# Another written order of an attention and mixer kernel: the second batch's sums of values go ahead of the first channel mix, and twelve clamps and three scalings run on GpSimd

## The chip, the cores and the metric

One core of a Trainium2 chip runs the kernel. The metric is the device time of one execution in microseconds, the median of several runs.

## The reference, cut to what matters

Linear attention (4 batches, 4 heads, 1088 rows, 32 columns a head) feeds a mixer: a token mix over the 1088 rows, then a channel mix from 128 to 1536 columns and back, each with a residual.

```python
def phi(x):                       # r = 8, so 64 features from 32 columns
    a = np.einsum('rd,bhsd->bhsr', S1, x)
    b = np.einsum('rd,bhsd->bhsr', S2, x)
    return np.einsum('bhsi,bhsj->bhsij', a, b).reshape(*x.shape[:-1], r * r)
q_p, k_p = (phi(q), phi(k))
kv = np.einsum('bhsf,bhsd->bhfd', k_p, v)
z = np.sum(k_p, axis=2)
num = np.einsum('bhsf,bhfd->bhsd', q_p, kv)
den = np.einsum('bhsf,bhf->bhs', q_p, z)[..., None] + 1e-06
x = (num / den).transpose(0, 2, 1, 3).reshape(B, S, H * D)
h = np.maximum(x.transpose(0, 2, 1) @ w_tok1, 0.0) @ w_tok2
u = x + h.transpose(0, 2, 1)
return u + np.maximum(u @ w_ch1, 0.0) @ w_ch2
```

## The kernel before, in words

**The order.** The program first adds some 1050 operations to a plan, each with the engines that may run it, and then emits them in the order of the string `ORDER` (`Plan.run`). An entry `w02.clamp:pool` names an operation and, behind the colon, its engine (`dve` is VectorE, `act` ScalarE, `pool` GpSimd; without one, the first engine that the operation lists). Each engine works through its own instructions in this order, so an entry's place counts only against entries of the same engine: TensorE, VectorE, ScalarE, GpSimd, or SP, which issues the loads (`d00` alone is issued by ScalarE) and all other transfers. Semaphores between the engines are set from what the instructions read and write. Tiles rotate through a fixed number of buffers in the order of the string (`ps_a` 3 PSUM banks, `ps_h` 3, `ps_o` 2, `o_sb` 2), so an operation that takes a buffer waits until the last reader of the tile before in it is done.

**The weights.** They arrive as 64-bit floats and are converted on the core. Weight 0 is `w_tok1` in six pieces (256, 256, 512, 512, 512 and 256 columns), 1 is `w_tok2` in six (384 four times, 320 twice), 2 and 3 are `w_ch1` and `w_ch2` in four each (256, 256, 512, 512). `dWI` loads piece I of weight W. Then `convert` runs six operations: `abs` scales the high words into `c` (L270 on VectorE or GpSimd, L272 on ScalarE), `low` turns the low words into `tail` (L276, ScalarE), `sign` takes the sign bits (L281 on ScalarE, into a bank of `ps_h`; L284 on VectorE, in place), `clamp` bounds `c` (L287), `merge` joins `c` and the sign (L290, VectorE), `add` adds `tail` (L294, L296, GpSimd). `hi` and `lo` (L377 ScalarE, L380) split a piece into two halves that TensorE multiplies at its fast rate; pieces of weights 2 and 3 need them before the channel mix, those of 0 and 1 before batch 1's token mix. `s` is the same for S1 and S2.

**A batch.** `qB`, `kB`, `vB` load the inputs. `K.p0`, `p4` project the keys (L407), `K.c0`, `c4` copy one factor (L418, ScalarE), `K.v0`, `v4`, `v8` form the products (L428, VectorE: 1024, 1024 and 256 columns), and `K.s` sums values over them (L448: 72 short matmuls as six operations for batch 0, 144 as one for the others); `K.kvz` copies the sums (L457). `Q0` projects and multiplies batch 0's queries on the chip (`p`, `a`, `m`: L537, L559, L569); for the others `Q.p` projects (L497), `Q.c0`, `c1` copy, `Q.w0`, `w1` write the rows to DRAM, `Q.r..` read them back spread out, and `Q.m..` multiply (L632). `A.x` attends (L652, 24 short matmuls a third; batch 0 as `x0` to `x2`), `A.d0` to `d2` divide (L663, L664, L666, VectorE), `A.t0` to `t2` are the first token matmuls (L702 or L708), `A.relu` (L720), `A.hT` transposes (L742), `A.hTh`, `hTl` split, `A.u0` to `u2` put x into the bank (L733, batch 0), `A.w0` to `w2` are the second token matmuls (L824 or L828); for batches 1 to 3 x goes through DRAM (`xb`, `xm`, `xT`) and `us` adds it. `A.uhIK` and `A.ulIK` split u into halves for span K (L799, L802).

**The channel mix.** The 4352 rows are cut into 12 spans, `U0` to `U11`, of 384, 320 or 288. A span has 12 blocks of 128 hidden columns, and each block four operations: `f`, three matmuls into a bank of `ps_h` (L878); `h`, the relu to `hh` (L882, ScalarE); `l`, the rest `hl` (L885, VectorE), which frees the bank; `s`, three matmuls into the span's bank of `ps_o` (L891). `U2.f#4` below is the fourth block's `f`. `oh`, `ol` and `out` add u and store. `f` of blocks 1 and 2 needs piece 20, of 3 and 4 piece 21, of 5 to 8 piece 22, of 9 to 12 piece 23; `s` the same of weight 3.

**Fills.** `fill:n` emits n bfloat16 matmuls of 512 columns that nobody reads (L248); eight stand ahead of the whole string. Before the change the string has seven.

## Time and profile before

| | us |
|---|---|
| three runs | 217.52, 217.95, 216.55 |
| their median | 217.52 |
| the profiled execution | 218.62 |
| its span, first to last instruction | 216.8 |

The profile is of one execution. Times in it are from the span's start; the other 1.8 us of that execution lie around the span. PE is TensorE's matmuls, PEld its weight loads, which overlap them; DVE is VectorE, ACT ScalarE, POOL GpSimd. A matmul of two 32-bit operands shows as two records. A granted clock of 1.00 is 2.4 GHz on TensorE, and matmuls at half of it take twice their time.

### The profile page before, as it was taken

The page shows a single profiled execution, that of the slowest core. Times are in us where ns is not written, and L with a number is a line of the kernel's source. Part 1 is how long each engine was busy: PE and PEld are TensorE (multiplying, and loading weights), DVE is VectorE, ACT ScalarE, POOL GpSimd, SP SyncE. Part 2 cuts the span into 40 slices and gives each one's busy share as a digit, 9 for nine tenths or more (in the row PEclk, how much of TensorE's full clock was granted, in tenths as well). Part 3 has the DMA queues.
Part 4 walks back from the last instruction along what each step waited for, and adds up shares of the span by engine and source line. Part 5 has one row for each costly group of instructions (what it writes and reads, how often), then busy time and mean ns, then how long its engine had stood idle before and what let it go on. Part 6 is the DMA issues. An engine that isn't in the chain of part 4 may idle for free.

```text
span 216.8 us, 5259 instructions
## 1 busy us (share of the span) xinstructions
PE 209.7 (97%) x2069; PEld 195.0 (90%) x2069; DVE 144.9 (67%) x305; ACT 118.7 (55%) x282; POOL 64.5 (30%) x73
## 2 busy tenths in 40 slices
...
PEclk9999999799999999999999999999999999999999
...
GB/s 229 399 407 399 402 357 204 194 179 248 29 216 242 197 165 17 108 186 238 182 101 0 3 3 60 172 61 0 30 5 2 42 36 3 24 0 0 51 0 54
DMA packets 11472, 28.44 MB, mean 131 GB/s; under 512 B 1336, under 2 KB 5432, under 8 KB 11448
## 3 DMA queue, kind: packets, MB, share of 16 engines
...
q8 instruction: 16, 0.26, 0.5%
q10 hardware_dynamic: 144, 0.26, 0.4%
...
## 4 chain that ended last, share of the span: by engine, by line
PE 87%; DMA 4%; DVE 2%; issue 2%; SPq 2%; ACT 1%; ACTq 0%
PE ps_h L878 34%; PE ps_o L891 33%; DMA doubles<-wt 4%; PE ps_a L708 4%; PE ps_a L828 4%; PE ps_a L652 3%; PE ps_a L448 2%; PE ps_a L824 2%; SPq L252 1%; PE ps_a L702 1%; PE ps_a L407 1%; DVE c L290 1%; PE ps_a L497 1%; DVE k_p L428 1%; PE ps_a L733 1%
## 5 line engine op out<-in xcount | busy, mean ns | idle before, releaser
L885 DVE SCALAR_TENSOR_TENSOR hl<-ps_h,hh 128x384 fp32r<-128x384 f32 (+2 forms) x144 | 74.9, 532 | 59.6 <-ACT hh L882 58.5
L882 ACT ACTIVATE hh<-ps_h 128x384 fp32r<-128x384 f32 (+2 forms) x144 | 67.7, 475 | 75.4 <-PE ps_h L878 54.5
L878 PE MATMUL ps_h<-uh,halves 128*128 128x384 f32 (+2 forms) x288 | 87.6, 335 | 0.0
L891 PE MATMUL ps_o<-hh,halves 128*128 128x384 f32 (+2 forms) x288 | 71.5, 330 | 0.0
L878 PEld LDWEIGHTS ps_h<-uh,halves 128*128 128x128 f32 x288 | 53.8, 190 | 1.0 <-ACT hh L882 0.4
L891 PEld LDWEIGHTS ps_o<-hh,halves 128*128 128x128 f32 x288 | 50.6, 189 | 0.2
L878 PE MATMUL ps_h<-ul,halves 128*128 128x384 f32 (+2 forms) x144 | 47.7, 331 | 0.0
L891 PE MATMUL ps_o<-hl,halves 128*128 128x384 f32 (+2 forms) x144 | 47.3, 328 | 0.0
L878 PEld LDWEIGHTS ps_h<-ul,halves 128*128 128x128 f32 x144 | 27.4, 190 | 0.2 <-DVE ul L802 0.2
L891 PEld LDWEIGHTS ps_o<-hl,halves 128*128 128x128 f32 x144 | 27.2, 189 | 0.0
L802 POOL TENSOR_TENSOR ul<-us,uh 128x320 fp32r<-128x320 f32 (+3 forms) x8 | 6.6, 821 | 57.6 <-ACT uh L799 47.4
L294 POOL TENSOR_TENSOR whole<-c,tail 128x384 int32<-128x384 int32 (+3 forms) x12 | 11.8, 995 | 9.1 <-DVE c L290 7.8
L676 POOL TENSOR_TENSOR xl<-x,xh 128x384 fp32r<-128x384 f32 x7 | 7.1, 1019 | 22.6 <-ACT xh L672 22.6
L632 POOL TENSOR_TENSOR qp<-qp,br 128x544 f32<-128x544 f32 x8 | 10.9, 1369 | 6.2 <-PE ps_o L891 4.5
L428 DVE TENSOR_TENSOR k_p<-ps_a,a_sb 128x1024 f32<-128x1024 f32 (+1 forms) x12 | 11.4, 950 | 0.5 <-ACT a_sb L418 0.4
L276 ACT ACTIVATE tail<-doubles 128x256 int32<-128x256 uint32 (+3 forms) x20 | 10.9, 552 | 0.7 <-DMA doubles<-wt 0.7
L652 PEld LDWEIGHTS ps_a<-kvz,qp 128*64 128x64 f32 x288 | 8.9, 137 | 2.0 <-issue 0.9
L652 PE MATMUL ps_a<-kvz,qp 128*64 128x66 f32 x288 | 9.8, 223 | 0.5 <-issue 0.3
L290 DVE SCALAR_TENSOR_TENSOR c<-c,ps_h 128x512 int32<-128x512 int32 (+3 forms) x17 | 9.3, 559 | 1.1 <-ACT ps_h L281 0.8
L708 PE MATMUL ps_a<-halves,xh 128*128 128x256 f32 x54 | 9.9, 280 | 0.0
L281 ACT ACTIVATE ps_h<-doubles 128x512 int32<-128x512 f32 (+3 forms) x17 | 9.2, 543 | 0.0
L380 POOL TENSOR_TENSOR halves<-whole,halves 128x384 fp32r<-128x384 f32 (+3 forms) x7 | 8.1, 1177 | 2.4 <-ACT halves L377 2.4
...
## 6 DMA issues: line engine op xcount, KB each, us to landing
...
```

Of the source, the lines that this page charges most:

```text
L276: nc.scalar.activation(t["tail"], low.bitcast(U32), AF.Copy, scale=2.0 ** -29)
L281: nc.scalar.activation(t["sign"], f32(high), AF.Prelu, scale=2.0 ** -19, alpha=2.0 ** 70)
L290: nc.vector.scalar_tensor_tensor(t["c"], t["c"], 3, t["sign"], op0=ALU.logical_shift_left, op1=ALU.bitwise_or)
L294: engines[e].tensor_tensor(dst(), t["c"], t["tail"], op=ALU.add)
L428: nc.vector.tensor_tensor(t["k_p"][:pn, t0 * H:t1 * H], a.unsqueeze(3).broadcast_to([pn, n, R, R]), t["sb", base][:pn, at:at + n].unsqueez ...
L632: engines[e].tensor_tensor(qp[:, p, cs], qp[:, p, cs], t["br"][:, p, cs], op=ALU.mult)
L652: nc.tensor.matmul(x_ps[c:c + 64, o:o + 2 * (D + 1)], lhsT=qp[:, p, s0 + c:s0 + c + 64], rhs=kvz_all[b % 2][:, p, :], start=True, stop=True,)
L708: nc.tensor.matmul(t["h_ps"][:, :DTOK], lhsT=t[l][:m, i, :], rhs=part(0, piece, r, j * DTOK, DTOK)[:m], start=(i == 0 and k == 0), stop=(i ...
L878: nc.tensor.matmul(h_ps[:, :cn], lhsT=part(2, at[2][e][0], l, at[2][e][1] * P, P), rhs=r[:, :cn], start=(m == 0), stop=(m == 2))
L882: nc.scalar.activation(t["hh"][:, :cn], t["h"][:, :cn], AF.Relu)
L885: nc.vector.scalar_tensor_tensor(t["hl"][:, :cn], t["h"][:, :cn], 0.0, f32(t["hh"][:, :cn]), op0=ALU.max, op1=ALU.subtract)
L891: nc.tensor.matmul(outs[i][:, :cn], lhsT=part(3, at[3][e][0], l, at[3][e][1] * P, P), rhs=r[:, :cn], start=(e == 0 and m == 0), stop=(e == ...
```

## The change

Only the string `ORDER` is changed. The work is the same but for the fills, of which the string now has nine, one at a time but for the first four, and for the engines of some operations:

- Scalings (`abs`): w02 goes from GpSimd to ScalarE; w00 from VectorE, w10 and w23 from ScalarE to GpSimd; w01 and w33 from VectorE to ScalarE; w03, w13, w22 and w31 from ScalarE to VectorE.
- Clamps: w01, w10, w03, w04, w13, w11, w32, w14 and w23 go from VectorE to GpSimd, w00 and w33 from GpSimd to VectorE; with w02, w05 and w20, which stay there, GpSimd has twelve.
- Signs: those of s, w00 and w15 go to ScalarE, of w01 and w23 to VectorE; Q0.s0 goes from GpSimd to VectorE.
- Halves: `lo` of w22, w23, w13, w05 and some of the later `A.l` and `A.ul` go to VectorE; `lo` of w00, w04 and w12, some `A.ul` and Q3.m00, m01 go to GpSimd; `oh` of spans 0 and 2 goes to GpSimd, of span 1 to VectorE.

On TensorE K1.s now stands between A0.w0 and A0.w1, ahead of the first U0.f; A0.x0 ahead of Q1.p; K1.p0 and p4 between A0.t0 and A0.t1; A0.u2 behind the first U0.f. On SP the order of the loads changes: k0 ahead of d10 and v0, d14 to the end with d33, and v1 behind Q1.w0 but ahead of d32, d23, q2 and d15. Cut to the part up to the second batch, and the end:

```diff
--- before.py
+++ after.py
@@ -61,53 +61,53 @@
 ORDER = """
-d00 s d10 q0 s.low s.abs w00.low w00.abs:dve s.sign:dve s.clamp s.merge s.add w00.clamp:pool Q0.s0:pool w00.sign:dve w00.merge w00.add w10.abs:act
-w10.low Q0.s1:act d01 w10.clamp:dve w10.sign:act w10.merge w01.abs:dve w10.add w01.low fill:4 Q0.p00 Q0.p01 Q0.a00 Q0.a01 w01.sign:act Q0.m00 Q0.m01
-w01.clamp:dve w01.merge Q0.p20 Q0.a20 k0 d02 K0.p0 K0.p4 Q0.p21 K0.c0 s.rows w02.abs:pool w02.clamp:pool K0.c4 w02.low Q0.a21 d04 w02.sign:act v0
-K0.v0 Q0.m20 K0.v8 Q0.m21 K0.v4 d03 q1 d05 fill:2 Q0.p10 Q0.p11 K0.s00 K0.s04 K0.s08 K0.s10 K0.s14 K0.s18 w04.abs:act Q0.a10 Q0.a11 w04.low w01.add
-w02.merge w02.add w04.clamp:dve Q0.m11 Q0.m10 w03.abs:act w03.low w04.sign:act K0.kvz w03.clamp:dve w05.abs:dve w05.clamp:pool w04.merge w03.sign:act
-Q1.p d13 w03.merge Q1.c0 w05.low Q1.c1 w13.abs:act w05.sign:act w13.low w13.sign:act A0.x0 w04.add d11 d12 d30 d20 k1 d21 d22 d14 d31 d32 q2 d23 v1
-Q1.w0 Q1.w1 d15 d33 w03.add A0.d0 A0.x1 w13.clamp:dve w05.merge A0.d1 w13.merge w05.add A0.x2 A0.t0 A0.d2 A0.t1 A0.t2 w11.abs:act w11.low w12.low
-w12.abs:act w30.abs:act w11.sign:act w30.low w12.sign:act w30.sign:act A0.relu w13.add K1.p0 A0.hT K1.p4 w11.clamp:dve w20.abs:dve w12.clamp:dve
-w30.clamp:dve w11.merge w12.merge w30.merge w20.clamp:pool w11.add w20.low K1.c0 w20.sign:act w12.add w30.add w21.abs:act w21.low K1.c4 A0.hTh
-w21.sign:act w22.low w30.hi K1.v0 w20.merge w20.add w20.hi w20.lo:pool w22.abs:act K1.v4 w21.clamp:dve w30.lo:dve K1.v8 w21.merge fill:1 A0.u0 A0.u1
-A0.w0 A0.w1 A0.uh00 w22.sign:act w31.abs:act A0.ul00 w22.clamp:dve w14.abs:dve U0.f U0.f Q2.p w21.add w21.hi w21.lo:pool w22.merge w22.add A0.uh11
-A0.ul11 U1.f U0.h w31.low U0.l U0.h U0.l w32.low w32.abs:act w31.clamp:dve w31.sign:dve w14.clamp:dve w32.clamp:dve w31.merge U1.h w22.hi w32.sign:act
-U1.l w32.merge w31.add w14.low w31.hi w14.sign:act Q2.c0 U0.s U0.s w14.merge K1.s U0.f U0.f U1.s w22.lo:pool w31.lo:pool w32.add U0.h w15.low U0.h
...
-U10.h U10.l U10.h U10.l U11.f U11.f U10.s U11.h U11.l U11.h U11.l U11.h U11.l U11.f U10.s U11.h U11.l U11.f U11.s U10.f U11.s U10.f U11.s U11.s U11.h
-U11.l U10.h U10.l U10.h U10.l U10.f U10.h U10.l U11.f U11.s U10.s U11.f U11.f U10.s U11.h U11.l U10.s U11.f U11.h U11.h U11.h U11.l U11.l U10.ol U11.l
-U11.s U11.f U11.h U11.s U11.s U11.s U11.l U11.s U11.ol U10.out U11.out
+d00 s q0 d01 k0 s.abs s.low s.sign:act w00.low s.clamp w00.abs:pool w00.clamp:dve s.merge s.add Q0.s0:dve Q0.s1:act w00.sign:act s.rows w01.abs:act
+w01.low w00.merge fill:4 Q0.p00 Q0.p01 Q0.a00 Q0.a01 Q0.p20 Q0.a20 d10 w01.clamp:pool w01.sign:dve w01.merge Q0.m00 Q0.m01 K0.p0 K0.p4 Q0.p21 K0.c0
+Q0.a21 w10.low K0.c4 K0.v0 K0.v4 w01.add w00.add w10.abs:pool w10.clamp:pool fill:1 Q0.p10 v0 d02 w10.sign:act d05 d03 d04 w10.merge K0.v8 Q0.m21
+w05.abs:dve Q0.m20 K0.s00 K0.s04 K0.s08 K0.s10 K0.s14 K0.s18 Q0.p11 q1 d12 d13 k1 d11 w02.abs:act w02.low Q0.a11 w02.sign:act w03.low Q0.a10 w10.add
+w02.clamp:pool w05.clamp:pool K0.kvz w05.low w04.abs:act w02.merge w03.abs:dve Q0.m10 Q0.m11 w05.sign:act w03.sign:act w04.low fill:1 A0.x0 A0.d0
+fill:1 Q1.p Q1.c0 Q1.c1 w04.sign:act w03.clamp:pool w05.merge w02.add w04.clamp:pool A0.x1 w03.merge w05.add w03.add A0.d1 w04.merge w12.abs:act
+w13.abs:dve w12.clamp:dve w13.clamp:pool w13.low w12.low w13.sign:act w12.sign:act A0.x2 A0.t0 A0.d2 d21 d20 d30 d31 d22 Q1.w0 v1 d32 d23 q2 d15 Q1.w1
+d14 d33 Q1.r0None Q1.r00 Q1.r01 Q1.r1None Q1.r10 Q1.r11 fill:1 K1.p0 K1.p4 w04.add w13.merge K1.c0 w11.low w11.abs:act K1.c4 w11.sign:act w12.merge
+K1.v0 w13.add w11.clamp:pool w20.abs:dve w12.add w20.clamp:pool w20.low w20.sign:act w30.low w30.abs:act A0.t1 A0.t2 A0.relu fill:1 A0.hT w21.low
+w11.merge w11.add K1.v4 w20.merge K1.v8 w20.add A0.hTh A0.u0 A0.u1 A0.w0 K1.s A0.w1 w30.sign:act w20.hi w21.abs:act w22.abs:dve w30.clamp:dve
+w30.merge w22.low w21.sign:act w31.low A0.uh00 w22.sign:act w20.lo:pool w21.clamp:dve w31.abs:dve w22.clamp:dve w31.clamp:dve w31.sign:dve w30.add
+K1.kvz w30.hi w32.low A0.uh11 w21.merge A0.ul00 w21.add w22.merge w31.merge w30.lo:dve U0.f A0.u2 U0.f A0.ul11 U0.h w32.abs:act U0.h w22.add
+w32.clamp:pool w31.add U0.l U1.f U1.f U0.l U0.s U0.s U1.h w21.hi w21.lo:pool U1.l U1.h w22.hi U1.l U1.s U0.f Q2.p U1.s w22.lo:dve w14.abs:dve
+w15.abs:dve w32.sign:act w31.hi w14.low U0.h w32.merge U0.l w14.clamp:pool w31.lo:pool w15.clamp:dve w14.sign:act w15.low w15.sign:act w14.merge U0.f
+w15.merge U0.s U1.f U1.f U0.h U1.h U0.l w32.add w14.add w15.add U1.l U0.f U0.s U0.f U1.h U1.l U0.h w05.hi w32.hi U0.l U0.h w23.low w02.hi Q2.c0 w04.hi
+U0.l w23.abs:pool w23.clamp:pool w23.sign:dve w23.merge w23.add U1.s U1.f U1.s A0.w2 U1.f U1.h w32.lo:dve U0.f U1.l Q1.m00:pool U0.s U1.s U0.f U0.s
+A0.uh22 U1.h Q2.c1 w33.low U1.l U0.h A0.ul22 U0.l U1.f U1.s U1.f U0.s w23.hi U0.h w23.lo:dve U0.l U0.f w13.hi U1.h U1.l Q1.m10:dve w33.abs:act w11.hi
+U1.h U0.h w00.hi w01.hi w33.clamp:dve U1.l U0.l U1.f U0.s U1.s U1.s U1.h w33.sign:act U1.l U0.f U1.f Q1.m01:dve Q1.m11:pool w33.merge w03.hi w15.hi
+U0.h U1.h w33.add w33.hi w33.lo:pool w04.lo:pool w02.lo:pool A1.x U1.l U0.l w01.lo:dve A1.d0 A1.d1 A1.d2 A1.xb U0.f U0.f U2.f U0.s U1.s U1.s U0.s
+Q2.w0 Q2.w1 v2 k2 q3 Q2.r0None Q2.r00 A1.xm Q2.r01 A1.xT0 A1.xT1 A1.xT2 Q2.r1None A1.xT3 Q3.p U0.h U0.h Q3.c0 A1.h0 U0.oh:pool w00.lo:pool w03.lo:pool
...
+U9.ol U9.out U11.f U10.s U11.f U11.h U11.l U10.s U11.f U11.h U11.l U11.s U11.h U11.l U11.f U11.f U11.s U11.s U11.f U11.h U11.l U11.h U11.l U11.h U11.l
+U11.s U10.f U11.f U11.s U11.s U11.f U10.h U10.l U11.h U11.l U11.h U11.l U10.f U10.f U11.s U10.s U10.h U10.l U10.h U10.l U11.s U11.f U10.s U11.f U11.f
+U10.s U11.h U11.h U11.l U11.l U11.f U11.h U11.h U11.l U10.ol U11.l U11.s U11.s U11.s U11.s U11.ol U10.out U11.out
 """.split()
```

## Rows read from the trace of the kernel before

**Rows 1.** The page's head: busy us (share of the span) and instructions of each engine, and the granted clock in 40 slices, in tenths.
```profile
PE 209.7 (97%) x2069; PEld 195.0 (90%) x2069; DVE 144.9 (67%) x305; ACT 118.7 (55%) x282; POOL 64.5 (30%) x73
...
PEclk9999999799999999999999999999999999999999
```
**Rows 2.** The cut into stretches: length in us, then each engine's busy us and instructions, the granted clock, the DMA engines' busy share and GB/s.
```profile
25.00:30.00 5.00, 4.80 (x38) 3.18 (x39) 4.80 (x10) 5.00 (x15) 4.33 (x6) 1.00 1.02 401
30.00:35.00 5.00, 4.99 (x170) 3.91 (x168) 4.78 (x13) 5.00 (x12) 2.76 (x4) 1.00 0.70 253
35.00:40.00 5.00, 3.37 (x18) 3.33 (x19) 2.21 (x5) 3.02 (x8) 3.95 (x4) 0.75 0.95 205
...
50.00:210.00 160.00, 160.00 (x1501) 157.29 (x1500) 102.58 (x211) 75.61 (x178) 37.21 (x34) 1.00 0.29 81
```
**Rows 3.** The waits of TensorE: who waited for whom, us in total, times, longest.
```profile
PE ps_a L448 <- issue: 1.6, 1, 1.6
```
**Rows 4.** The chain that ended last, in order of time, around K1.s: start us, us, what, and how many instructions.
```profile
33.47 1.52 PE ps_a L448 x125
34.99 1.64 issue
36.89 1.63 PE ps_h L878 x6
38.52 0.96 PE ps_o L891 x3
39.48 1.77 PE ps_h L878 x6
41.25 1.06 PE ps_o L891 x6
```
**Rows 5.** Instructions of TensorE: the stretch from the first to the second stall of "issue" (as rows 2), the queue that carries its instructions (packets, MB, share of 16 engines), and its timeline at the sums of batches 2 and 3.
```profile
19.11:34.99 15.88, 15.47 (x253) 11.35 (x252) 15.33 (x37) 14.90 (x38) 10.49 (x14) 1.00 0.93 355
...
q8 instruction: 16, 0.26, 0.5%
...
72.61 1.66 PE L448 MATMUL ps_a<-v_sb,k_p 128*32 128x33 f32 x144
...
119.58 1.43 PE L448 MATMUL ps_a<-v_sb,k_p 128*32 128x33 f32 x144
```
**Rows 6.** The timeline of TensorE, 10 to 32 us: start us, us, what, how many; in brackets an idle time ahead of it and what ended that.
```profile
10.75 0.60 PE L248 MATMUL ps_o<-warm 128*128 128x512 bf16 x2
...
13.15 2.29 PE L448 MATMUL ps_o<-v_sb,k_p 128*64 128x33 f32 x72
...
16.58 2.23 PE L652 MATMUL ps_a<-kvz,qp 128*64 128x66 f32 x59 [0.16 <-ACT kvz L457]
19.11 0.57 PE L652 MATMUL ps_a<-kvz,qp 128*64 128x66 f32 x13 [0.30 <-issue]
...
21.38 2.96 PE L702 MATMUL ps_a<-whole,x 128*128 128x256 f32 x12 [0.21 <-DVE x L666]
...
24.89 0.44 PE L742 MATMUL ps_a<-ident,h 128*128 128x128 f32 x2
25.25 0.80 PE L407 MATMUL ps_a<-s_c,k_sb 128*64 128x64 f32 x20
...
26.58 0.88 PE L733 MATMUL ps_a<-ident,x 128*128 128x128 f32 x6 [0.20 <-DVE k_p L428]
27.30 2.75 PE L824 MATMUL ps_a<-whole,hTl 128*128 128x384 f32 x8
29.58 0.63 PE L878 MATMUL ps_h<-uh,halves 128*128 128x384 f32 x1
...
31.01 0.69 PE L497 MATMUL ps_a<-q_sb,s_rows 64*32 64x272 f32 x16
```
**Rows 7.** Groups of instructions by line and shape: count, busy us in all, mean ns of one, and idle us ahead of them.
```profile
L428 DVE TENSOR_TENSOR k_p<-ps_a,a_sb 128x1024 f32<-128x1024 f32 x8 | 9.7, 1218 | 0.5 <-ACT a_sb L418 0.4
...
L287 DVE TENSOR_SCALAR c<-c 128x512 f32<-128x512 f32 x5 | 2.4, 471 | 0.0
...
L270 POOL TENSOR_SCALAR c<-doubles 128x512 f32<-128x512 f32 x1 | 1.5, 1529 | 1.8 <-DMA doubles<-wt 1.8
...
L287 POOL TENSOR_SCALAR c<-c 128x512 f32<-128x512 f32 x2 | 1.2, 615 | 1.5 <-DVE c L270 1.4
...
L380 DVE TENSOR_TENSOR halves<-c,halves 128x512 fp32r<-128x512 f32 x1 | 1.1, 1053 | 0.0
```
**Rows 8.** The timelines of ScalarE at K0.c0, of VectorE from 16 to 20 us (two merges of 512 columns, the three instructions of A0.d0, the clamp of w13) and of GpSimd beside it (two adds of 512).
```profile
9.55 0.27 ACT L418 COPY a_sb<-ps_a 128x128 f32<-128x128 f32 x1 [0.43 <-PE ps_a L407]
...
16.56 1.28 DVE L290 SCALAR_TENSOR_TENSOR c<-c,ps_h 128x512 int32<-128x512 int32 x2
17.76 0.17 DVE L663 TENSOR_SCALAR den<-ps_a 128x12 f32<-128x12 f32 x1
17.96 0.23 DVE L664 RECIPROCAL rec<-den 128x12 f32<-128x12 f32 x1
18.22 0.56 DVE L666 TENSOR_TENSOR x<-ps_a,rec 128x384 f32<-128x384 f32 x1
18.69 1.37 DVE L287 TENSOR_SCALAR c<-c 128x384 f32<-128x384 f32 x1
...
17.33 2.52 POOL L294 TENSOR_TENSOR whole<-c,tail 128x512 int32<-128x512 int32 x2 [0.19 <-DVE c L290]
```

55 lines of the change are left out of this document (24 added, 31 removed).

## The prediction

> **What bounds the kernel now.** I read the page's head first: TensorE has work in 209.7 us, 97% of the span, with the clock granted in full in all but one of the 40 slices [rows 1]. The cut into stretches shows where the other microseconds are. From 50 to 210 us TensorE is busy 160.00 of 160.00, so nothing can be won there, while VectorE (102.6), ScalarE (75.6) and GpSimd (37.2) have room. Before 50 us one stretch stands out, 35 to 40: 3.37 busy us and a granted clock of 0.75 [rows 2]. TensorE's waits name what happened: the longest is 1.6 us, in the sums of values K1.s (L448), put down to "issue", so to no semaphore [rows 3]. The chain in order of time shows its consequence: 1.52 us of sums, 1.64 us of nothing, then 15 matmuls of the first channel mix in 1.63 + 0.96 + 1.77 = 4.36 us, where at full clock six take 1.06 and 15 some 2.6 [rows 4]. So a stall of 1.64 us and 1.76 us from matmuls at 1.2 instead of 2.4 GHz: 3.40 us lie there.
>
> **Why it stalls there.** A stall of "issue" comes twice: 0.30 us in A0.x at 19.11 and 1.64 us at 34.99 [rows 4, 6]. Between them lie 253 matmuls and 252 weight loads, 505 instructions; the queue of TensorE's instructions moves 16 packets, 0.26 MB, for 4138 of these, so a packet is some 16 KB or 256 instructions with the semaphores [rows 1, 5]. 505 are two packets. My reading: both stalls stand where a block of code ends and the next had not come. K1.s is 288 instructions in about 1.5 us, so here it ran through a whole block alone. The boundary between the two stalls, 253 instructions before the second, lies a dozen matmuls into K1.s, at 33.5; the code after it was there at 36.63, 3.1 us later. One block before the first stall is 0.65 us into K0.s, 13.8: that code took 5.3 us [rows 6]. The same 144 sums of batches 2 and 3 run in 1.66 and 1.43 us without a stall [rows 5]; there only one boundary falls inside, by the same count.
>
> **Part by part.**
>
> *A, K1.s ahead of the first mix: -3.40 us, if nothing takes the stall's place.* I count TensorE's instructions up to K1.s in both orders: 672 before, 606 after. The boundary that lay 23 instructions into K1.s then lies 89 into it, and the next one 54 instructions behind its end, in U1.s#1. Between them TensorE has 1.1 us of sums, A0.w1 1.0, A0.u2 0.3 and seven groups of three matmuls at 0.52: 6.0 us, against code that took 3.1 and 5.3. The 5.3 fell in the full load of weights, and so will this (DMA share 1.02 at 25 to 30 us [rows 2]), so it is the nearer row and leaves 0.7. I take the whole 3.40; bounds 0 (a stall as long somewhere) and -3.40.
>
> *B, when the first mix begins: +0.4 us.* Now U0.f starts at 29.58 with K1.s (1.5 us) still to come, so an equal start behind K1.s is 31.1. I walk the new order from where both are alike, with durations of [rows 6 to 8], smaller tiles by their columns. Behind K0.c0 (done at 9.82 [rows 8]) VectorE has K0's products 1.22 + 1.22, w10.merge 0.55 and 0.42: 13.2. On TensorE the sums that need the last product take 1.2, Q0.p11 1.0, a fill 0.25, A0.x0 0.93: 16.6. A0.d0 is 0.17 + 0.23 + 0.56 = 0.96: 17.6. Then VectorE does w05.merge 0.41, w03.merge 0.68, d1, w04.merge 0.68, w13.abs 0.49, w12.clamp 0.34, d2: 22.1. K1.p4 needs the PSUM bank that d2 frees, and stands ahead of A0.t1 and t2: 22.1 + 0.75 + 3.0 = 25.85; relu beside a fill, and hT 0.44: 26.65. A0.u1 waits for the bank of K1.v8: VectorE has from 22.1 two merges 1.1, products 1.22 + 1.22 + 0.42, w20.abs 0.28, w11.merge 0.55, w20.merge 0.41: 27.3. Then u1 0.35, w0 1.3, K1.s 1.5, w1 1.0: U0.f at 31.45. I take 0.4 late; bounds -0.2 (queues that overlap better than the walk) and +1.6 (both added fills, 0.60 us [rows 6], exposed, and 0.3 on each of four links). Late next is VectorE, 4.8 of 5 us busy here already [rows 2].
>
> *C, new waits in the first mix: +0.75 us.* ScalarE's signs take turns with the mix for three ps_h banks. U0.f#4 gets the bank of w32.sign, free when VectorE has merged w32. From the end of U1.l#1 VectorE has U1.l#2 0.55, w22.lo (new on VectorE: 0.68 by columns to 1.05 by its row), w14.abs and w15.abs 0.3 each, w32.merge 0.68: 2.5 to 2.9; TensorE has U1.s#1, U0.f#3, U1.s#2 at 0.52 and Q2.p 0.69: 2.25. That is a wait of 0.3 to 0.65 with U0.s#3 queued behind it, and for both their own h and l. Then U1.f#3 needs w14 merged: U0.l#3 0.55, w15.clamp 0.32, w14.merge 0.49 against two groups, 1.04: 0.3 more. Together 0.6 to 0.95, I take 0.75; bounds 0 (w22.lo done early) and 0.95, without what the clock may add (a rival).
>
> *The moves between engines: 0.* Nine clamps leave VectorE for GpSimd and two (w00, w33) come back. At 0.47 for 512 columns VectorE is relieved of some 2.5 us; GpSimd takes 0.62 for 512 [rows 7]. Of the scalings w02 leaves GpSimd, and w00, w10, w23 come; one of 256 or 384 columns is not in the trace there. The clamp of 512 (0.62), taken by columns, bounds it below, the scaling of 512 (1.53) above; I take 0.8 and 1.15, by columns from the latter. GpSimd's room hides this: 4.3 and 2.8 of 5 us busy [rows 2]. The narrow point is w04.add, which A0.t2 needs. From w10.merge (12.7) GpSimd has five adds (w10 1.0, w02 1.3, w05 0.73, w03 and w04 1.26 each [rows 8]) and six clamps (3.3, by columns): 8.8, so 21.5, and t2 starts at 24.35. The cover is 2.8 us; gone, all of it shows. Signs and halves that swap engines go between queues with room: 0, bounds 0 and 0.5.
>
> *The later order and SP's queue: 0, bounds 0 and +1.0.* v1 goes behind Q1.w0 but ahead of d32, d23, q2 and d14: 1.75 MB less ahead of it, 4.4 us sooner at 401 GB/s [rows 2]; it is there by 33.4 now, so by 29.0, when K1.s wants it. d14 goes near the end of the loads; w14.abs asks for it near 36. A1.xm goes ahead of Q2.r01, Q2.r1None ahead of A1.xT3; this delays Q2's products on GpSimd, which has room. TensorE waits for nothing after 50 us, so such slips eat slack first; 1.0 is a wait of one group twice. At the end U10.ol goes ahead of the last U11.l, half a microsecond beside four groups of 0.4.
>
> **The sum.** -3.40 + 0.40 + 0.75 = -2.25 us. Against the profiled execution (218.62 us, of which 216.8 are its span) that is 216.4. That execution lies 1.1 above the median of the runs, 217.52; from there the forecast is 215.3 us.
>
> **A page on the stall.** The Trainium skill, "Runtime: NRT & Kernel Launch", "Instruction fetch mechanics", has the same block of 256 instructions, but says that fetching hides behind the pace at which instructions are dispatched. By that rule the 1.64 us would not be code and would go where K1.s goes, the first rival; two stalls just two blocks apart speak against it.
>
> **The rivals.**
> - *The stall belongs to the burst and moves with it:* A is 0, so +1.15, 218.7 us. For it: it stands in K1.s. Against: two like bursts without one [rows 5].
> - *The code comes late once more,* in U1.s#1: at 7 us instead of 5.3 a stall of 1.0 and the clock's 1.76, so +0.5, 218.0. For it: 0.7 us of cover. Against: 5.3 is the longest that a row gives. It decides from 6.0.
> - *The waits of C drop the clock:* the 1.76 come back, 217.0. For it: a stall ahead of 15 slow matmuls [rows 4]. Against: waits of 0.2 and 0.3 us left no mark [rows 6].
> - *GpSimd becomes the bound of the conversion* (the other side). VectorE's w13.clamp took 1.37 us, where one of 512 averages 0.47, while GpSimd ran an add to 19.85 [rows 7, 8]. If GpSimd's six clamps ahead of w04.add each wait 0.9, so 5.4, w04.add comes 2.6 late, TensorE stands, the clock falls: 2.6 + 1.76 - 2.25 = +2.1, 219.6. It decides from 0.55 per clamp, where cover and gain are gone.
> - *Better:* B and C at nothing, 214.1.
>
> A page speaks for the fourth: the Trainium skill, "SBUF — State Buffer", "Who interferes with whom", has VectorE and GpSimd lock a shared port for whole instructions. The 1.37 us agrees; but it cuts both ways, since clamps off VectorE no longer meet GpSimd's adds.
>
> **Chances.** Forecast 0.40 (its own range 214.6 to 216.1), better 0.20, clock 0.14, late code 0.10, burst 0.06, GpSimd 0.10. A measurement here tells about 1%, 2.2 us, from no change. Faster by that, under 215.3: the better case and somewhat over half of the forecast, 0.43. Slower, over 219.7: half of the GpSimd case, and late code or a later stage that cost more than priced, 0.10. Same: 0.47. The range leaves out the low end of the better case and the high end of the last: 213.7 to 218.7.
>
> **What would show it.** Right: K1.s in one piece near 29 to 31 us, no "issue" over 0.3 us from 20 to 50, a granted clock of 1.00 from 35 to 45, the first U0.f at 31.2 to 31.8, a wait of 0.3 to 0.7 before U0.f#4, and TensorE unbroken after 50. Wrong: an "issue" stall at another block's end, a clock under 1.00, w04.add after 24 us, or waits after 50.

## The result, and the profile after

The changed order takes 218.81 us (median of 10 runs, 218.21 to 219.66) against 217.59 for the kernel before beside it (10 runs, 216.55 to 222.46). The ratio is 1.0058, 95% interval 1.0036 to 1.0080: slower by some 1.25 us where I forecast 2.2 faster, and a tenth above the upper end of my range. Here and below a ratio leaves out executions over 1.5% above the fastest of their kernel (63 of the 146 that the kernel before made beside the experiments, each at a mean granted clock of 0.992 or less, and none of the ten of the changed order), so a ratio does not weigh these, and the median of all runs can stand away from it.

The profiled execution of after took 219.26 us. The head of its page, as in [rows 1]:

```profile
PE 209.5 (96%) x2071; PEld 193.4 (89%) x2071; DVE 144.4 (66%) x303; ACT 117.0 (54%) x280; POOL 66.4 (31%) x77
...
PEclk9999999999999999999999999999999999999999
```

The stretches of [rows 2]:

```profile
25.00:30.00 5.00, 4.61 (x23) 3.04 (x21) 4.89 (x11) 4.49 (x13) 4.37 (x7) 1.00 1.03 408
30.00:35.00 5.00, 4.79 (x159) 3.68 (x158) 4.89 (x10) 4.05 (x11) 2.68 (x3) 1.00 0.99 311
35.00:40.00 5.00, 4.69 (x36) 3.55 (x36) 4.63 (x11) 4.92 (x12) 3.12 (x5) 1.00 0.68 207
...
50.00:210.00 160.00, 159.27 (x1492) 156.22 (x1491) 103.02 (x215) 75.15 (x178) 32.95 (x30) 1.00 0.31 84
```

From 35 to 40 us TensorE has 4.69 busy us at full clock, not 3.37 at 0.75: what the change was to remove is gone. But the quiet 160 us behind it now hold 0.73 us without work. TensorE's waits, as in [rows 3]:

```profile
PE ps_o L248 <- DVE warm L229: 1.0, 1, 1.0
PE ps_a L537 <- ACT xT L559: 0.8, 1, 0.8
PE ps_a L652 <- issue: 0.8, 1, 0.8
PE ps_o L891 <- DVE o_sb L910: 0.7, 1, 0.7
PE ps_h L878 <- DVE ul L802: 0.5, 1, 0.5
```

The wait of 1.6 on "issue" in L448 has gone, and K1.s runs in one piece (30.18, 1.57 us). The first row is the start and is there before as well. The other four are new: two at the start (Q0.p20, A0.x0), U2.s#1 at 71 us, U1.f#1 at 35. What each stands behind is read below.

To find where the time lies, four starts were read from each trace: K0.p0, the first U0.f, A1.x, the last U11.s. "Again" is a second profiled execution of before (216.76 us).

| us | before | again | after |
|---|---|---|---|
| K0.p0 starts | 8.81 | 8.97 | 9.58 |
| to the first U0.f | 20.77 | 20.48 | 23.20 |
| on to A1.x | 26.64 | 24.88 | 22.73 |
| on to the last U11.s | 156.79 | 156.85 | 158.15 |
| the last U11.s starts | 213.01 | 211.18 | 213.66 |

### The profile page after: what moved, and what is told of

Same layout as the page of the kernel before. It is cut to its first block, busy times and chain, and to the rows that moved or that the text cites. A ratio compares the mean times of both kernels' runs of the same rounds, so it can differ in the third digit from the quotient of the medians.

```text
span 217.5 us, 5255 instructions
## 1 busy us (share of the span) xinstructions
PE 209.5 (96%) x2071; PEld 193.4 (89%) x2071; DVE 144.4 (66%) x303; ACT 117.0 (54%) x280; POOL 66.4 (31%) x77
## 4 chain that ended last, share of the span: by engine, by line
PE 86%; DVE 7%; DMA 3%; ACT 2%; issue 1%; SPq 0%; DVEq 0%
PE ps_o L891 33%; PE ps_h L878 32%; PE ps_a L652 4%; PE ps_a L828 4%; PE ps_a L708 3%; DMA doubles<-wt 3%; DVE halves L380 2%; PE ps_a L702 2%; PE ps_a L407 2%; PE ps_a L448 1%; PE ps_o L448 1%; DVE hl L885 1%; PE ps_a L537 1%; PE ps_h L537 1%; DVE c L290 1%
## 5 line engine op out<-in xcount | busy, mean ns | idle before, releaser
L878 PE MATMUL ps_h<-uh,halves 128*128 128x384 f32 (+2 forms) x288 | 85.9, 333 | 0.0
L878 PEld LDWEIGHTS ps_h<-uh,halves 128*128 128x128 f32 x288 | 52.9, 188 | 1.0 <-DVE hl L885 0.5
L802 POOL TENSOR_TENSOR ul<-us,uh 128x64 fp32r<-128x64 f32 (+3 forms) x6 | 4.1, 684 | 55.2 <-ACT uh L799 38.2
L632 POOL TENSOR_TENSOR qp<-qp,br 128x544 f32<-128x544 f32 x10 | 14.8, 1499 | 11.0 <-DMA br<-rows 11.0
L428 DVE TENSOR_TENSOR k_p<-ps_a,a_sb 128x1024 f32<-128x1024 f32 (+1 forms) x12 | 11.2, 948 | 0.3 <-ACT a_sb L418 0.3
L296 POOL TENSOR_TENSOR c<-c,tail 128x256 int32<-128x256 int32 (+1 forms) x8 | 8.7, 1085 | 7.6 <-DVE c L290 6.2
L380 POOL TENSOR_TENSOR halves<-whole,halves 128x512 fp32r<-128x512 f32 (+3 forms) x8 | 8.7, 1100 | 1.2 <-ACT halves L377 1.2
```

Source lines behind the costliest of these rows:

```text
L380: engines[e].tensor_tensor(halves[w, i][:, 1], f32(whole[w, i] if w < 2 else t["c"]), f32(halves[w, i][:, 0]), op=ALU.subtract)
L428: nc.vector.tensor_tensor(t["k_p"][:pn, t0 * H:t1 * H], a.unsqueeze(3).broadcast_to([pn, n, R, R]), t["sb", base][:pn, at:at + n].unsqueez ...
L632: engines[e].tensor_tensor(qp[:, p, cs], qp[:, p, cs], t["br"][:, p, cs], op=ALU.mult)
L878: nc.tensor.matmul(h_ps[:, :cn], lhsT=part(2, at[2][e][0], l, at[2][e][1] * P, P), rhs=r[:, :cn], start=(m == 0), stop=(m == 2))
```

## The experiments

**The stall once more, moved, and the sums moved alone.** The kernel before without an edit:

> The kernel before, profiled once more. Theory (the stall in K1.s and the half clock vary from execution to execution with the load on the transfer queues, and the execution of the profile, 1.1 us above the median, had a long one): a stall of 0.3 to 1.3 us and less at half clock. Rival: 1.6 us again and the same 15 slow matmuls.

Measured: 216.76 us. TensorE's timeline at K1.s:

```profile
33.27 1.68 PE L448 MATMUL ps_a<-v_sb,k_p 128*32 128x33 f32 x138
36.29 0.26 PE L448 MATMUL ps_a<-v_sb,k_p 128*32 128x33 f32 x6 [1.35 <-issue]
36.48 0.44 PE L878 MATMUL ps_h<-uh,halves 128*128 128x384 f32 x1
```

The stall is there again, 1.35 us, but what follows runs at full clock:

```profile
35.00:40.00 5.00, 3.71 (x26) 3.67 (x27) 2.54 (x6) 3.65 (x10) 3.83 (x4) 1.00 0.92 206
```

So the half clock of [rows 2, 4], 1.76 us of my sum, belongs to some executions only. The stall of 1.35 us lies just above the 0.3 to 1.3 expected. The next edit leaves the order and moves the ends of TensorE's blocks of code, by 116 instructions:

```diff
-WARM = 8
-PAD = 0
+WARM = 6
+PAD = 60       # so many tiny matmuls ahead of the string
```

> The kernel before, with 60 tiny matmuls (32 weight columns, 8 columns of data, nobody reads them) ahead of the written order and six warm-up fills for eight. Nothing else moves; TensorE's 120 added instructions shift where its code blocks end: the boundary that lay 23 instructions into K1.s comes about 95 ahead of it, and the next falls inside K1.s. Theory (the 1.64 us are code that comes late, and the half clock follows from them): no 'issue' stall over 0.3 us in K1.s, clock 1.00 from 35 to 45 us, and 2 to 3.4 us less than before, less up to 1 us that the tiny matmuls cost. Rival (the stall belongs to the burst of 144 sums): the same stall and the same time.

Measured: 219.38 us, ratio 1.0088 [1.0053, 1.0123]. K1.s ran unbroken (34.62, 1.95 us to its end), and a stall of 1.4 us on "issue" stood in K2.s, where by the count two blocks now ended. From K0.p0 to A1.x it took 44.44 us, 0.92 less than in "again", and from there to the last U11.s 158.91, 2.06 more: the stall was moved, not saved, and the time missed the expected gain. Then K1.s and v1 moved, and nothing else:

```diff
-A0.w0 A0.w1 ... d31 d32 q2 d23 v1 ... w14.merge K1.s U0.f
+A0.w0 K1.s A0.w1 ... v1 d31 d32 q2 d23 ... w14.merge U0.f
```

> The kernel before with one part of the change alone: K1.s between A0.w0 and A0.w1 as in the changed kernel, and v1 loaded ahead of d31 so that it is there. Theory (this part is worth what the prediction said, and the loss of the changed kernel comes from the rest of the order): no stall in K1.s, clock 1.00, first U0.f about 1.5 us later, and 1.5 to 3.4 us less than before. Rival (the part itself is worth nothing, because the mix that starts later waits as long): within 0.5 us of before.

Measured: 217.46 us, ratio 1.0014 [0.9972, 1.0056]: nothing gained. K1.s has no stall, but the first mix now waits:

```profile
30.93 1.42 PE L448 MATMUL ps_a<-v_sb,k_p 128*32 128x33 f32 x144 [0.21 <-PE ps_a L824]
...
38.14 0.44 PE L878 MATMUL ps_h<-uh,halves 128*128 128x384 f32 x1 [0.67 <-DVE hl L885]
```

From K0.p0 to A1.x it took 45.74 us, "again" 45.36. (This execution, 219.63 us, lies above its median: the first product stood 1.96 us for its load, the clock was granted at half from 9.0 to 12.4 us, and K0's projections took 1.91 us against 1.27 in "again", so some 0.6 of the 45.74 are the clock's.) My reading was that K1.s inside the mix had been work for TensorE while VectorE and ScalarE got the next blocks ready.

**The start of after.** ScalarE's timeline, 6 to 9 us, and TensorE's beside it:

```profile
7.68 0.43 ACT L272 ACTIVATE c<-doubles 128x256 f32<-128x256 f32 x1 [1.03 <-DMA doubles<-wt]
8.02 0.41 ACT L276 ACTIVATE tail<-doubles 128x256 int32<-128x256 uint32 x1
8.34 1.16 ACT L559 COPY xT<-ps_a 128x384 f32<-128x384 f32 x3
```
```profile
8.84 0.80 PE L537 MATMUL ps_a<-q_sb,s_spread 64*128 64x320 f32 x2 [0.82 <-ACT xT L559]
```

w01.abs waits 1.03 us for its load, and Q0.a00, whose bank Q0.p20 needs, stands behind it. Likewise K0.kvz, which A0.x0 needs, stands behind w02.sign and w03.low.

```diff
-w02.sign:act w03.low Q0.a10 ... K0.kvz w05.low
+Q0.a10 w02.sign:act ... K0.kvz w03.low w05.low
```

> The changed kernel with one reordering on ScalarE: Q0.a10 goes ahead of w02.sign, and w03.low behind K0.kvz. Theory (A0.x0 stood still for 0.8 us because K0.kvz was queued on ScalarE behind conversions that waited for their loads and for a PSUM bank): A0.x0 starts 0.7 to 0.8 us sooner, first U0.f about 0.7 sooner, and 0.5 to 0.8 us less than the changed kernel. Rival (the conversion chain to A0.t2 sets the start anyway): the first U0.f where it was, no gain.

Measured: 218.53 us, ratio 1.0048 [1.0016, 1.0080]. A0.x0 came 0.28 us behind its fill, not 0.78, and A0.x1 then waited 0.80 for A0.d0, not 0.27: the wait moved one step on.

```diff
 s.rows
-w01.abs:act w01.low w00.merge fill:4 Q0.p00 ... Q0.a20 d10 w01.clamp:pool w01.sign:dve w01.merge Q0.m00 Q0.m01
+w00.merge fill:4 Q0.p00 ... Q0.a20 w01.abs:act w01.low d10 w01.clamp:pool Q0.m00 Q0.m01 w01.sign:dve w01.merge
...
-... Q0.m10 Q0.m11 ... A0.x0 A0.d0
+... A0.x0 A0.d0 Q0.m10 Q0.m11      # and the edit above
```

> The kernel after with the start undone by order alone: on ScalarE Q0.a00, Q0.a01 and Q0.a20 ahead of w01.abs and w01.low (so no copy of a query waits for the load d01), Q0.a10 ahead of w02.sign and K0.kvz ahead of w03.low; on VectorE w01.sign and w01.merge behind Q0.m01 and A0.d0 ahead of Q0.m10 and Q0.m11. Theory (U0.f#1 came at 32.78 and not at the 31.45 that I forecast because ScalarE's queue put loads ahead of the chain of the keys): Q0.p20 without a wait, A0.x0 at about 15.8 and A0.x1 about 1.3 us behind it, U0.f#1 at 30.9 to 31.5, time 0.8 to 1.5 us lower, about 217.6. Rival (TensorE's first 30 us are set by the merges and additions of the weights w02 to w05 on GpSimd, which stay where they are): A0.x1 or A0.t1 to A0.t2 wait instead, U0.f#1 at 32.0 or later, time lower by less than 0.4.

Measured: 222.87 us, ratio 1.0203 [1.0146, 1.0261]. Q0.p20 no longer waited, and the first U0.f came at 36.22. With w01 later, w10's scaling on GpSimd came later (11.66 us, 11.03 in after), so its merge on VectorE, so K0.v8 behind that (13.95, 13.34), while the sums that need it began sooner (12.04, 12.73):

```profile
14.42 2.35 PE L448 MATMUL ps_o<-v_sb,k_p 128*64 128x33 f32 x40 [1.26 <-DVE k_p L428]
...
18.83 1.59 PE L652 MATMUL ps_a<-kvz,qp 128*64 128x66 f32 x24
```

After this wait of 1.26 us the 24 matmuls of A0.x0 took 1.59 us (0.92 in after), and the cut shows half the clock:

```profile
15.00:20.00 5.00, 5.00 (x61) 3.42 (x61) 1.69 (x4) 3.29 (x8) 3.07 (x6) 0.50 1.02 400
```

With the two edits that follow below, and two fills less, it came out alike:

> The kernel after with the three edits of this call together, and without two of its nine fills (the one ahead of Q1.p and the one ahead of K1.p0). If the three losses are each what they seem in the profile and independent, the time falls by 0.6 + 0.7 + 1.1 + 0.3 = 2.7 us to about 216.1, and the ratio to the kernel before is 0.990 to 0.996: the move of K1.s then gives what its stall cost, about 1.4 us, and no more. Rival (the losses hide one another, or the kernel after has a floor near that of before): ratio 0.997 to 1.003.

Measured: 220.74 us, ratio 1.0111 [1.0058, 1.0164], with the same wait of 1.26 for K0.v8 and a clock of 0.56 and 0.50 in the ten us behind it. The start buried what the other edits gave, so this run tells nothing of their sum.

**The late output of span 0.** VectorE of after, 66 to 72 us, and TensorE's wait:

```profile
66.35 2.46 DVE L380 TENSOR_TENSOR halves<-whole,halves 128x320 fp32r<-128x320 f32 x2
68.73 0.94 DVE L885 SCALAR_TENSOR_TENSOR hl<-ps_h,hh 128x320 fp32r<-128x320 f32 x2
69.59 1.54 DVE L428 TENSOR_TENSOR k_p<-ps_a,a_sb 128x1024 f32<-128x1024 f32 x2
71.06 0.54 DVE L910 TENSOR_TENSOR o_sb<-o_sb,ps_o 128x384 f32<-128x384 f32 x1
```
```profile
71.65 0.56 PE L891 MATMUL ps_o<-hh,halves 128*128 128x320 f32 x2 [0.73 <-DVE o_sb L910]
```

U0.ol (L910) frees the bank that U2.s#1 needs. Its sums ended at 65.9, but it is queued behind w15.lo and w05.lo (2.46 us in all), two blocks' `l`, and K2.v0 and v8.

```diff
-U2.f K2.v0 K2.v8 A1.relu U0.ol K2.v4
+U2.f U0.ol K2.v0 K2.v8 A1.relu K2.v4
```

> The kernel after with U0.ol ahead of K2.v0 on VectorE, nothing else. Theory (U2.s#1 waited 0.73 us at 70.9 because U0.ol, ready from 65.9, stood behind four VectorE instructions, two of them stretched to 1.30 and 1.24 us): no wait at U2.s#1 above 0.1, time 0.6 to 0.8 us lower, about 218.1. Rival (the bank is not what decides; the next stage, K2.s with K2.v0 and K2.v8 1.2 us later on VectorE, waits instead): the wait reappears at K2.s or U1.s#12, time unchanged within 0.2 us.

Measured: 217.48 us, ratio 0.9980 [0.9953, 1.0008], and the wait is gone:

```profile
68.83 0.54 DVE L910 TENSOR_TENSOR o_sb<-o_sb,ps_o 128x384 f32<-128x384 f32 x1
```
```profile
70.00 0.45 PE L891 MATMUL ps_o<-hh,halves 128*128 128x320 f32 x2
```

From A1.x to the last U11.s it takes 157.06 us, 1.09 less than after. That is more than the 0.73, since the profile counts the matmul ahead of the wait as work up to its modelled end: from the start before it to its own, U2.s#1 takes 0.15 us here and 1.04 in after. With this one entry moved, the loss against the kernel before can no longer be told.

**The first mix: two causes, one behind the other.** VectorE of after from 32.9 us, and GpSimd's w22.add beside it:

```profile
32.94 0.42 DVE L290 SCALAR_TENSOR_TENSOR c<-c,doubles 128x256 int32<-128x256 int32 x1
33.28 1.51 DVE L380 TENSOR_TENSOR halves<-c,halves 128x256 fp32r<-128x256 f32 x1
34.71 0.55 DVE L802 TENSOR_TENSOR ul<-ps_a,uh 128x384 fp32r<-128x384 f32 x1
```
```profile
33.10 1.40 POOL L296 TENSOR_TENSOR c<-c,tail 128x512 int32<-128x512 int32 x1 [0.33 <-DVE c L290]
```

w30.lo took 1.51 us; in before it took 0.42:

```profile
28.10 0.42 DVE L380 TENSOR_TENSOR halves<-c,halves 128x256 fp32r<-128x256 f32 x1
```

It ended 0.29 us after GpSimd's add, and A0.ul11, which U1.f#1 needs, stood behind it. The Trainium skill, "SBUF — State Buffer", "Who interferes with whom", has VectorE and GpSimd share one pair of ports under an exclusive lock. The two rows of after agree with it.

```diff
-w31.merge w30.lo:dve U0.f
+w31.merge w30.lo:pool U0.f
```

> The kernel after with one tag changed: w30.lo runs on GpSimd, ahead of w22.add, not on VectorE. Theory (the first mix lost time because VectorE's w30.lo, 0.42 us elsewhere, was held for 1.51 us while GpSimd's w22.add ran, so A0.ul11 and with it U1.f#1 came 0.8 late): w30.lo takes 0.7 to 0.8 us on GpSimd from about 32.8, A0.ul11 follows w31.merge at once, the wait of U1.f#1 on A0.ul11 falls from 0.8 to under 0.2, and the time falls by 0.5 to 0.8 us, to about 218.1. Rival (U1.f#1 is late because of the whole row of VectorE's instructions ahead of it, whichever engine has w30.lo, or the lost time comes back at the next wait): the wait stays above 0.4 or moves to U0.s#1 or U1.f#2, time 218.6 to 219.

Measured: 218.68 us, ratio 1.0042 [0.9999, 1.0084]: no gain that can be told. The wait of U1.f#1 is gone, U0.s#1 comes 3.87 us behind A0.w1, not 4.73, and by U0.f#8 all but 0.08 of that is lost (16.90, 16.98). Some 0.5 of it is lost in U1.s#1, the rest between U0.f#4 and U1.f#3:

```profile
35.87 0.34 PE L891 MATMUL ps_o<-hh,halves 128*128 128x384 f32 x1
36.65 0.33 PE L891 MATMUL ps_o<-hh,halves 128*128 128x384 f32 x1 [0.44 <-issue]
```

This is "issue" again, behind 946 of TensorE's instructions (473 matmuls, and a weight load for each). The next kernel sets eight instructions ahead of everything.

```diff
-PAD = 0
+PAD = 4        # and w30.lo:pool
```

> The kernel after with w30.lo on GpSimd (as e5_lo) and four tiny matmuls, eight instructions of TensorE, ahead of everything. Theory of the block of code: the stall of 0.44 us, which stood behind the first matmul of U1.s#1, comes eight instructions sooner in the order, at the first matmuls of U0.s#2, and ends at the same distance from K1.s. Rival (it belongs to U1.s#1, its weights or its halves): it stays behind the first matmul of U1.s#1.

Measured: 218.91 us. The stall is now at the first matmul of U0.s#2:

```profile
35.39 0.34 PE L891 MATMUL ps_o<-hl,halves 128*128 128x384 f32 x1
36.87 0.51 PE L891 MATMUL ps_o<-hh,halves 128*128 128x384 f32 x2 [1.14 <-ACT halves L377]
```

(The profile puts this down to a split of weights on ScalarE, L377. The one that U0.s#2 reads, w30.hi, had ended at 32.13, 4.7 us before; the last one before the matmul, w22.hi, ended at 36.36, but in e5 the same matmul ran at 35.36, ahead of w22.hi's end at 36.15.) Eight instructions of shift, and the stall stands eight sooner, again behind 946. Two more kernels, the second the first with `w30.lo:pool`, have two fills less, so four instructions less:

```diff
-fill:1 Q1.p ... fill:1 K1.p0 ... Q0.m10 Q0.m11 ... A0.x0 A0.d0 ... K2.v0 K2.v8 A1.relu U0.ol
+Q1.p ... K1.p0 ... A0.x0 A0.d0 Q0.m10 Q0.m11 ... U0.ol K2.v0 K2.v8 A1.relu   # and the edit of K0.kvz
```

> The kernel after with U0.ol ahead of K2.v0; Q0.a10 ahead of w02.sign, K0.kvz ahead of w03.low on ScalarE and A0.d0 ahead of Q0.m10 and Q0.m11 on VectorE (without the edit of w01 that made TensorE wait for K0.v8); and without the fills ahead of Q1.p and K1.p0. Theory (the after kernel loses some 1.0 us at U0.ol, 0.8 at A0.x0 and A0.x1, and 0.3 for each fill on the path): U0.f#1 at 31.2 or sooner when K0.p0 is at 8.8, no wait over 0.3 at A0.x1 and U2.s#1, time 216.6 to 217.0, ratio 0.993 to 0.997, the first version of the new order that beats the kernel before. Rival (the first mix waits for the conversion, whenever it begins): U0.f#1 comes sooner, U0.f#8 doesn't, time 217.4, ratio 0.998.

> The kernel of the run above (e10_after) with w30.lo on GpSimd as well. If the block of code that begins some 948 instructions into TensorE's program is what holds the first mix (it stood for 0.44 us in U1.s#1 when w30.lo alone was moved), the time is that of e10_after within 0.3 us, with a stall of issue of 0.3 to 0.7 us in U1.s#1 or U0.f#3 in place of the wait of U1.f#1. If the wait for w30.lo is the bound, 0.6 to 0.8 us below e10_after.

Measured: 218.30 us, ratio 1.0058 [1.0015, 1.0102], and 217.72 us, ratio 1.0018 [0.9979, 1.0057]. The first missed: Q1.p waited 1.30 us for its query load and A0.x2 0.52 for ScalarE's copy of that projection (abT), in place of the waits that were taken out, and the first U0.f came at 32.70. In the second the wait for w30.lo is gone and the stall is at the first matmul of U0.f#3, for the third time behind 946:

```profile
36.62 0.34 PE L891 MATMUL ps_o<-hl,halves 128*128 128x384 f32 x1
37.48 0.34 PE L878 MATMUL ps_h<-uh,halves 128*128 128x384 f32 x1 [0.53 <-ACT halves L377]
```

Three kernels, three instructions, one count. TensorE had passed the block's end before that one, inside K1.s, 6.8 to 7.2 us earlier.

The sums alone were tried again with the idle time of ScalarE and VectorE used:

```diff
-w22.merge w22.add A0.uh11 A0.ul11 U1.f U0.h w31.low U0.l U0.h U0.l w32.low w32.abs:act w31.clamp:dve w31.sign:dve w14.clamp:dve w32.clamp:dve w31.merge
+w22.merge w22.add w31.low w32.low A0.uh11 w31.clamp:dve w31.sign:dve w14.clamp:dve w31.merge A0.ul11 U1.f U0.h U0.l U0.h U0.l w32.abs:act w32.clamp:dve
```

> The kernel before with K1.s ahead of A0.w1 and v1 ahead of d31 (the move of the sums alone, which gave 217.46 us and ratio 1.0014), and now six instructions of the conversion taken into the 1.3 us in which ScalarE and VectorE stood waiting for A0.w1: w31.low and w32.low ahead of A0.uh11 on ScalarE, w31.clamp, w31.sign, w14.clamp and w31.merge ahead of A0.ul11 on VectorE. Theory (the stall of 1.35 to 1.64 us in K1.s cost little of itself, because TensorE's sums were the cover under which the other engines prepared the first mix; moved ahead, the mix waits for them instead, 0.67 us at U0.f#3 and 0.2 to 0.3 at two other places): with the idle time used, U0.f#3 waits under 0.2 and the time falls by 0.6 to 1.0 us, to about 216.6, ratio 0.994 to 0.998. Rival (the waits of the first mix have other causes): U0.f#3 still waits over 0.4, ratio 1.000 to 1.003.

Measured: 218.61 us, ratio 1.0043 [1.0002, 1.0084]. U0.f#3 still waited 0.37, and 0.38 came at Q2.p for A0.ul11: a wait moved, none saved. My theory fell: the idle time was not usable by this edit, so that K1.s was cover for the other engines stays argued. (This profile too, 220.32 us, has half the clock from 7.8 to 11.2 us.)

**The blocks' ends moved, the order kept.**

```diff
-WARM = 8
-PAD = 0
+WARM = 5
+PAD = 98       # e13; 87 in e16, 130 in e18; in after's order 105 (e14, e15), 117 (e17)
```

Of the three in after's order, e14 and e17 also have `w30.lo:pool` and U0.ol ahead of K2.v0.

> The kernel before, its order untouched; of its eight warm-up matmuls three are replaced by 98 tiny ones (60 of these took 0.63 us), so that TensorE's program is 190 instructions longer ahead of the work and its blocks of code end 190 instructions earlier in the work. By the count that three kernels gave (a block ends at instruction 946 and every 253), K1.s then meets a block's end at its instruction 86 and the next one 6.8 us later in the first mix; K2.s and K3.s have 12 and 5 us. Theory (the stall is code, and is on the path: with 60 tiny ones the first mix behind K1.s went on without a wait, 1.88 us after the start of K1.s and not 3.2): no issue over 0.3 us at K1.s, K2.s, K3.s, time 1.2 to 1.6 us below the kernel before, ratio 0.992 to 0.996. Rival (the stall is cover for the conversion, which is what binds): the stall goes and waits of the first mix come in its place, ratio 0.998 to 1.002.

Measured: 217.41 us, ratio 0.9991 [0.9958, 1.0024]. K1.s ran unbroken (35.24, 1.85 us) and TensorE stalled some 6 us behind the block's end in it, in U1.f#4:

```profile
41.45 0.34 PE L891 MATMUL ps_o<-hl,halves 128*128 128x384 f32 x1
43.29 0.44 PE L878 MATMUL ps_h<-uh,halves 128*128 128x384 f32 x1 [1.50 <-issue]
```

> The kernel before, its order untouched, with the blocks of code ending 168 instructions earlier in the work (87 tiny matmuls in place of three of the warm-up's), not 190. With 190 the code that K1.s asked for came 7.7 us after it and TensorE stood 1.5 us in the first mix (U1.f#4), where it got in 6.4 us. With 168 the next block's end lies 8.8 us behind the one in K1.s; K2.s and K3.s leave 3.6 and 4.2 us, where the code took some 2.7 (the K2.s of 60 tiny ones, 1.3 us of sums and a stall of 1.4). Theory (the stall is on the path, about 1.35 us in most runs): no stall of issue over 0.3 us after 20 us, time 1.2 to 1.6 us below the kernel before, ratio 0.992 to 0.996. Rival (the mix would wait for the conversion in its place): ratio 0.998 to 1.002 with waits between 36 and 45 us.

Measured: 218.02 us, ratio 1.0016 [0.9980, 1.0053]. With 8.8 us between the ends no stall of "issue" over 0.3 us is left, K1.s to U0.f#3 takes 1.59 us and not 3.21:

```profile
34.26 1.66 PE L448 MATMUL ps_a<-v_sb,k_p 128*32 128x33 f32 x144
35.85 0.44 PE L878 MATMUL ps_h<-uh,halves 128*128 128x384 f32 x1
```

Of these 1.62 us the first mix gives 0.38 back by A1.x, in no single wait, and 0.69 had gone ahead of it, where TensorE now waits 0.46 for a query load at Q1.p and 0.71 for VectorE at A0.t1: K0.p0 to A1.x is 44.81 us against 45.36 of "again". The time did not show it. In this trace the first product stood 1.8 us for its query load (0.4 in "again"), and A1.x to the end took 0.41 more. The control has the stall back where it was:

> The kernel before, order untouched, with the blocks of code ending 254 instructions earlier (130 tiny matmuls in place of three of the warm-up's), a whole block, so that K1.s meets its two ends where the kernel before meets them: the control for e16_before_shift2, which has the same replacement of warm-up matmuls and no stall, and came out at 1.0016 [0.998, 1.0053]. If the stall is on the path and the replacement itself costs something (the query load came 1.7 to 1.9 us late in all three such kernels of this order), the stall is back in K1.s and the ratio is 1.006 to 1.010. If the stall is worth nothing, the stall is back and the ratio is that of e16, 1.000 to 1.003.

Measured: 223.38 us, ratio 1.0052 [0.9995, 1.0109]. By the ratios the difference to e16 is 0.36%, 0.8 us, less than either interval is wide: what the stall alone is worth in time stays open. The traces of before have 1.35 and 1.64.

> The kernel after with U0.ol ahead of K2.v0, w30.lo on GpSimd, and the blocks of code ending 204 instructions earlier in the work (105 tiny matmuls in place of three of the warm-up's). By the count the block's end in K1.s then leaves 9 us to the next one, against 6.9 now and about 7 that the code took. Theory (w30.lo and the code at instruction 946 hide one another: either edit alone gives nothing in the first mix, both give 0.8): no issue over 0.3 us in U0.s#2 to U0.f#3, U0.f#8 about 15.0 us behind A0.w1 and not 16.9 to 17.1, time 0.6 to 0.9 us below the kernel with U0.ol alone (217.48), so 216.7, ratio 0.991 to 0.996. Rival (the conversion of w22 and w32 binds the first mix): U0.f#8 stays 16.7 us or more behind A0.w1, ratio 0.997 to 1.000.

> The kernel after, order untouched, with the blocks of code ending 204 instructions earlier in the work (as in e14_after_shift). Theory: nothing, since U1.f#1 waits 0.8 us for A0.ul11 ahead of the old place of the block's end, and U2.s#1 for U0.ol; 218.5 to 219.0, ratio 1.004 to 1.008. Rival (the code late at instruction 946 is the whole loss): 0.8 us lower.

> The kernel after with U0.ol ahead of K2.v0, w30.lo on GpSimd, and the blocks of code ending 228 instructions earlier in the work (117 tiny matmuls in place of three of the warm-up's; 204 earlier gave 217.23 us). The places that a block's end leaves least time behind are then K1.s (8.0 us, code took 7.0 to 7.7) and K3.s (6.9); with 204 it was 9.3 and 4.0. Theory (with 204 all stalls of code were gone): the same time, 217.0 to 217.4. If the K3.s of 204 still lost something, 0.3 us lower.

Measured: e14 217.23 us, ratio 1.0000 [0.9982, 1.0017]; e15 218.89, 1.0082 [1.0056, 1.0109]; e17 217.10, 0.9981 [0.9962, 1.0001]. The shift alone gives nothing, w30.lo alone nothing; with both, and U0.ol, the first U0.f to A1.x takes 22.11 and 21.95 us against 22.73, and U0.f#8 comes 16.37 and 16.20 us behind A0.w1. (I had expected 15.0, the rival 16.7 or more; what the rest waits for was not read.) This gain of 0.6 to 0.8 us is seen in the traces alone: by their ratios neither can be told from e6, which has U0.ol alone (0.9980). The interval of the last version lies wholly below that of after. Against the kernel before it just reaches 1, so that it beats both is not shown.

## Why the prediction was wrong, step by step

- **What bounds the kernel, and why it stalls there: right.** Both readings of [rows 3 to 5] held: a stall where a block of TensorE's code ends, and code that is late when a second end follows too soon. That it goes with the count and not with the instruction is shown by the three stalls behind 946, by K2.s, and by U1.f#4. The trace of TensorE's instruction queue (the q8 of [rows 5]) agrees: in each of these stalls one packet of it lands 1.3 to 1.8 us before TensorE goes on. The Trainium skill, "Runtime: NRT & Kernel Launch", "Instruction fetch mechanics", holds such crossings to be mostly hidden; in this kernel's burst of 288 short instructions they were not, by 1.35 us and more.
- **A: right in kind, mis-sized.** "I take the whole 3.40" held for the profiled execution (K1.s 3.49 and half clock 1.76, against 1.57 now). It isn't what every execution holds: in "again" K1.s took 3.21 us and no half clock followed, so A is -1.64. Worse, the sum then came down by another 1.1 us because that execution lay above the median, and it lay there for the very 1.76 that I had just subtracted (first U0.f to A1.x: 26.64 against 24.88 in "again"). The same microseconds were taken off twice.
- **B: the step that failed first.** "From where both are alike" was not so at K0.c0 (10.31, against 9.55 in [rows 8]): Q0.a00 stood behind a load. And the walk from there followed VectorE and TensorE, not ScalarE, where K0.kvz stood behind w02 and w03, so A0.x0 began at 17.12, where the walk has it done at 16.6. K0.p0 to the first U0.f grew by 23.20 - 20.48 = 2.72, of which K1.s is 1.57: B is 1.15, and 0.61 more for the late K0.p0 in this execution, against 0.4. Its upper bound of 1.6 is not the sum of the parts named for it either: 0.60 and four times 0.3 are 1.8. No edit tried brought the loss back, so what binds the start stays open.
- **C: near in size, right in half of its places.** A whole K1.s of 3.21 left the stretch to A1.x, which shrank by 24.88 - 22.73 = 2.15, so the waits cost 1.06, against 0.75. Ahead of U0.f#4 some 0.3 to 0.4 went, as priced; ahead of U1.f#3 nothing; and U1.f#1 took 0.8 to 0.9 longer, for a w30.lo of 1.51 us that no term of mine held.
- **The rival "The code comes late once more" was real and hidden.** The block ends in U1.s#1, and in three kernels the code came 6.8 to 7.2 us after the end before it. After doesn't show it, because TensorE was already standing for A0.ul11: its packet landed at 36.14, and by the 1.3 to 1.8 us of the others (an estimate) the code was there between 37.4 and 37.9, when TensorE came to it. My cover of 6.0 was near; the nearer code of 5.3 was too short.
- **The moves between engines: right.** w04.add ran from 22.70 to 23.98, ahead of A0.t2 at 25.58; the rival with GpSimd as the bound fell. Sharing with GpSimd did cost, but through three lo on VectorE (w30, w15, w05), not through GpSimd's clamps. In VectorE's queue ahead of A0.ul11 two scalings that the change moved there were stretched as well, w22.abs to 0.94 us and w31.abs to 0.82, where like ones without GpSimd beside them took 0.42 and 0.29; what that cost was not tested.
- **The later order: the step that failed most.** "TensorE waits for nothing after 50 us, so such slips eat slack first": VectorE had the room on average and none at 71 us. It cost 158.15 - 156.85 = 1.30, more than its bound of 1.0, and e6 gave back 1.09 of it. I had looked for slips of transfers and did not ask, of each bank, where the instruction that frees it stands in its queue.
- **The sum again,** against "again": -1.64 + 1.15 + 1.06 + 1.30 = +1.87, and 0.61 for K0.p0, so 2.48 us, the difference of the two last rows. Against the medians it is 1.2: "again" lies 0.8 below the median of before, and the profiled execution of after 0.45 above its own. The range was narrower than its own terms: with A at 0 and B, C and the later order at their bounds the sum is +3.55, so 221.1 us, and 218.7 was no more than the burst rival alone. One part is argued only: the change issues q0 ahead of d10, and the first product began at 5.7 to 6.5 us in the twelve profiles of its order, at 6.4 to 8.0 in the eight of the order before. That should have helped the change; I had not priced it, and no run tried it alone.
